# Third pair's scores one slot sooner, last results in separate tiles, the first pair's subtraction and sums inside ScalarE's exponential

## The chip, the core and the metric

The kernel runs on one core of a Trainium2 chip. The metric is device time in microseconds (us), of one launch. A core has engines that run side by side, each in the order of its own instruction list: TensorE (PE in the profile; its weight loads are PEld), VectorE (DVE), ScalarE (ACT), GpSimd (POOL, hardly used here), and SyncE (SP), which here only issues transfers. Matmuls write to PSUM; VectorE and ScalarE read it from there.

## What is computed

A chunked attention followed by a feed-forward layer with the Mish function, in float32:

```python
# attention: q, k, v are (8, 8, 576, 64); chunks of 64 positions
scores = scale * np.matmul(q_c, k_c.transpose(0, 1, 2, 4, 3))
scores = scores - np.max(scores, axis=-1, keepdims=True)
attn = np.exp(scores)
attn = attn / (np.sum(attn, axis=-1, keepdims=True) + 1e-09)
x = np.matmul(attn, v_c)           # then laid out as (4608, 512)
# feed-forward: w_in (512, 2048), w_out (2048, 512)
h = x @ w_in
g = h * np.tanh(softplus(h))       # Mish
out = g @ w_out                    # (4608, 512)
```

## The kernel before

**Tiles.** The 4608 tokens are worked in nine blocks of 512 (`NB`), the 2048 inner columns in sixteen slices of 128 (`NF`), so there are 144 steps `i` = block * 16 + slice. A block needs the attention of two *pairs* `j` (256 tokens each, eight heads); pairs 0 and 1 feed block 0, pairs 2 and 3 block 1, and so on. In the text the third pair is `j` = 2 and the fourth is `j` = 3.

**Feed-forward.** `up(i)` (L288) makes `h` in PSUM with twelve matmuls: x and the weights are split into a high part and a small rest (`xh`, `xl`, `wi_h`, `wi_l`), and three of the four products are added up. `mish(i)` (L300, ScalarE) makes `z`; `g_hi` (L306 on ScalarE for even steps of block 0, else L308 on VectorE) and `g_lo` (L313, VectorE) split it into `gh` and `gl`. `down(i)` (L326) adds twelve matmuls into four accumulators `acc[t]` of 128 tokens, three for each. Per token group it takes `gl`, then `wo_l`, then `wo_h`. After the sixteenth slice `store` copies them out (L344, L346) and issues the transfers (L351).

**Weights.** They come as 64-bit numbers and are converted once, slice by slice, in the first 115 us: `w_load` (SyncE), `w_scale` (ScalarE, L89 and L93), `w_bits` (VectorE, two instructions, L99), `w_hi` (ScalarE, L114), `w_lo` (VectorE, L117). `order` lists the slices: index 2s + 3 is the output slice `o` of step s, index 2s + 4 the input slice `i` of step s + 3. `w_scale(0)` means the first of that list.

**Attention of a pair.** `a_scores` (TensorE, L162), `a_max` (VectorE, L189), `a_sub` (VectorE, L201, writes `p`), `a_exp` (ScalarE, L210, in place), `a_inverse` (VectorE: the sum L215, then + 1e-9 and the reciprocal, L216, L217), `a_norm` (VectorE, L222), `a_transpose` (TensorE, L231, into `pt`), `a_copy` (ScalarE, L241), `a_values` (TensorE, `av`), `a_hi` (ScalarE, L262, writes `xh`) and `a_lo` (VectorE, L265, writes `xl`). Exponential and Mish need different tables, so ScalarE loads a table (ACT_TABLE_LOAD) ahead of a change from one to the other.

**Order.** It is written out by hand. `prologue()` does pairs 0 and 1, each in two halves (FIRST, SECOND) so that one half can follow the other through the engines; `keep_busy(n)` puts in matmuls on the identity whose result nobody reads (L361). Then come slots `s` = 0 to 142. A slot issues on TensorE `up(s + 1)`, transposes, values and scores of whichever pair is due, then `down(s - 1)`; on VectorE and ScalarE the split of `z`, two weight slices (list indices 2s + 3 to 2s + 6 in various steps) and the attention steps that are due. In the slot's first half stand `a_max`, `a_norm`, `a_copy`, `a_exp`; in its second half, after `mish(s + 1)`, stand `a_sub`, `a_inverse`, `a_lo`. `plan` says in which slot a step of a pair is due: pair j has a base slot k0 (1 for pair 2, 8 for pair 3), and scores are due at k0, maximum and subtraction at k0 + 1, exponential and sum at k0 + 2, normalisation at k0 + 3, transposes and copy at k0 + 4, values at k0 + 5, `xh` and `xl` at k0 + 6. VectorE and ScalarE take what is listed strictly in order, so a step that waits holds all that is listed behind it.

**PSUM.** Scores, transposes and values of the pairs share one place (`HOME`, tag `a`); `ps_h` holds two tiles `h`; `ps_o` holds two tiles `o0` and `o2`, each with two accumulators. The prologue uses `o0` and `o2` as further places. In the last block `down` of the last two steps is interleaved by token group, with `store` behind each group:

```python
for i, t in ((2, 0), (2, 1), (1, 0), (2, 2), (1, 1), (2, 3), (1, 2), (1, 3)):
    down(N - i, (t,))
    if i == 1:
        store(NB - 1, (t,), end=True)
```

Of the kernel before, what the change touches and what calls it, by code (L numbers as in the profile page):

```python
# [9 lines left out]
F32 = mybir.dt.float32  # L10
# [7 lines left out]
P = 128  # L18
# [5 lines left out]
def kernel(  # L24
# [183 lines left out]
    def a_exp(j, t=BOTH):  # L208
        p = st[j]["p"][:, t]
        nc.scalar.activation(out=p, in_=p, func=AF.Exp, scale=SCALE)  # L210

    def a_inverse(j, t=BOTH):
        p = st[j]["p"][:, t].rearrange("p t g c k -> p (t g) c k")
        r = small(j, "r", t)
        nc.vector.tensor_reduce(out=r.rearrange("p c n -> p n c"), in_=p, op=ALU.add, axis=AX.X)  # L215
        nc.vector.tensor_scalar(out=r, in0=r, scalar1=1e-9, scalar2=None, op0=ALU.add)  # L216
        nc.vector.reciprocal(out=r, in_=r)  # L217

# [98 lines left out]
    def down(i, ts=range(TOK // P)):  # L317
        b, f = divmod(i, NF)
        d = it[i]
        for t in ts:  # L320
            if f == 0 and t % 2 == 0:
                o = ps_o.tile([P, 2, DM], F32, name=f"o_{b}_{t}", tag=f"o{t}")
                acc[t], acc[t + 1] = o[:, 0], o[:, 1]
            sl = slice(t * P, (t + 1) * P)
            for n, (g, w_) in enumerate(((d["gl"], wo_h), (d["gh"], wo_l), (d["gh"], wo_h))):
                nc.tensor.matmul(  # L326
                    acc[t],
                    lhsT=g[:, sl],
                    rhs=w_[:, f],
                    start=(f == 0 and n == 0),  # L330
                    stop=(f == NF - 1 and n == 2),
                )

    def store(b, ts=range(TOK // P), end=False):

        for t in ts:
            o = wst.tile([P, DM, 2], U32, name=f"ob_{b}_{t}", tag="st", bufs=4)
            o = o.rearrange("p n t -> p (n t)")[:, :DM].bitcast(F32)
            if end and t == TOK // P - 1:
                half = DM // 2  # L340
                nc.vector.tensor_copy(out=o[:, :half], in_=acc[t][:, :half])
                nc.scalar.copy(out=o[:, half:], in_=acc[t][:, half:])
            elif t % 2:
                nc.vector.tensor_copy(out=o, in_=acc[t])  # L344
            else:
                nc.scalar.copy(out=o, in_=acc[t])  # L346
            pair, c = divmod(t, 2)
            for i in range(2):
                r = (b * 2 * PAIRS + pair * 2 + i) * P + c * CHUNK
                queue = nc.scalar if end and i else nc.sync  # L350
                queue.dma_start(out=out[r : r + CHUNK, :], in_=o[i * CHUNK : (i + 1) * CHUNK])  # L351
# [13 lines left out]
    def prologue():  # L365
# [13 lines left out]
        for t, place in (FIRST, HOME), (SECOND, O0):  # L379
            keep_busy(7 if t == FIRST else 3)  # L380
            a_scores(0, t, place)
            a_max(0, t)
            a_sub(0, t)
            a_exp(0, t)
        w("scale", 0)
        for t, place in (FIRST, O2), (SECOND, HOME):
            a_inverse(0, t)
            a_norm(0, t)
            keep_busy(9 if t == FIRST else 3)
            a_transpose(0, t, place)  # L390
            a_copy(0, t)
        w("bits", 0)
        w("hi", 0)
        w("lo", 0)
        for t, place in (FIRST, O0), (SECOND, O2):
            a_values(0, t, place)
        for t in FIRST, SECOND:
            a_hi(0, t)
            a_lo(0, t)
        w("scale", 1)  # L400
        for t, place in (FIRST, HOME), (SECOND, O0):
            a_scores(1, t, place)
# [2 lines left out]
            a_exp(1, t)  # L405
        w("scale", 2)
        w("load", 4)
        up(0, A)
        for t, place in (FIRST, O2), (SECOND, HOME):
            a_inverse(1, t)  # L410
            a_norm(1, t)
            keep_busy(8 if t == FIRST else 4)
            a_transpose(1, t, place)
            a_copy(1, t)
        w("bits", 1)
        w("hi", 1)
# [16 lines left out]
        load_qk(2)  # L433
        w("load", 6)

    plan = {}
    for j in range(PAIRS, NPAIR):
        b, i = divmod(j, PAIRS)
        k0 = (b - 1) * NF + 1 + 7 * i
        for n in range(-2, 7):  # L440
            plan.setdefault(k0 + n, {})[n] = j

    def slot(s):
        a = plan.get(s, {})
# [1 line left out]

        if 1 <= s and s + 1 < N:
            up(s + 1, last="w")
        if 4 in a:
            a_transpose(a[4])  # L450
        if 5 in a:
            a_values(a[5])
        if 0 in a:
            a_scores(a[0])
        if 1 <= s <= N:
            down(s - 1)

# [5 lines left out]
        w("scale", n + 2)  # L463
        w("bits", n + 1)
        w("lo", n)
        if 1 in a:
            a_max(a[1])
        if 3 in a:
            a_norm(a[3])
        if 4 in a:  # L470
            a_copy(a[4])
        if 2 in a:
            a_exp(a[2])

        w("load", n + 5)
        if 6 in a:
            a_hi(a[6])
        if s + 1 < N:
            mish(s + 1)
        w("hi", n + 1)  # L480
        w("scale", n + 3)
        w("bits", n + 2)
        w("lo", n + 1)
        if 1 in a:
            a_sub(a[1])
        if 2 in a:
            a_inverse(a[2])
        if 6 in a:
            a_lo(a[6])
        if -2 in a and a[-2] > 2:  # L490
            load_qk(a[-2])
        if 1 in a:
            load_v(a[1])
        if s >= 1 and s % NF == 0:
            store(s // NF - 1)

# [49 lines left out]
```

## Time and profile before

| | us |
|---|---|
| three runs | 876.34, 876.52, 877.51 |
| median | 876.52 |
| the profiled execution | 877.21 |
| its span, first to last instruction | 875.4 |
| TensorE busy | 861.2 (98% of the span) |
| VectorE busy | 342.6 (39%) |
| ScalarE busy | 253.9 (29%) |

The profile is of one execution. Busy shares are means over the whole span; stage by stage they differ, and VectorE and ScalarE are far busier in the first 115 us, while the weights are converted, than after. In a row of the timeline the first number is the start in us from the beginning of the span, the second how long it lasted, then come engine, line of the kernel, operation, what it writes and reads, shapes, a count where rows are merged, and in brackets how long the engine stood idle before it and what released it.

### The profile page before, as it was taken

Reading aid. Unit: us, or ns where it says so; the run is one execution under the profiler, and the core shown is the slowest. Engines: PE = TensorE matmul, PEld = TensorE weight load, DVE = VectorE, ACT = ScalarE, POOL = GpSimd, SP = SyncE. Lnnn points to the kernel's source line nnn. Section 1 sums busy time; section 2 is a strip of 40 time slices with the busy share of each in tenths; the row PEclk is TensorE's granted clock in tenths of the full one; section 3 lists DMA queues with packets and bytes.
Section 4 is the critical chain, followed back from the end, with each engine's and each line's share of the span. In section 5 each row is a group of like instructions: output and inputs, shape, how many; then the busy total and the mean of one; then the engine's idle time right before and its main releaser. Section 6 shows DMA issues by size and latency. Waiting matters only on the chain.

```text
span 875.4 us, 13641 instructions
## 1 busy us (share of the span) xinstructions
PE 861.2 (98%) x5984; PEld 709.0 (81%) x5984; DVE 342.6 (39%) x534; ACT 253.9 (29%) x361; POOL 0.7 (0%) x6
## 2 busy tenths in 40 slices
PE   7989999999999999999999999999999999999997
PEld 7778888888888888888888888888888888888885
DVE  6898854242334233323424242423242242422221
ACT  4887832121312112221213131212222131311111
POOL 0000000000000000000000000000000000000000
PEclk9999999999999999999999999999999999999999
DMA  7656512101210120112120121012111202002001
GB/s 265 218 191 225 186 42 56 49 25 49 73 49 25 49 73 25 49 27 55 40 68 9 47 73 49 25 50 73 28 46 49 56 19 72 1 1 49 1 0 49
DMA packets 25179, 55.40 MB, mean 63 GB/s; under 512 B 2592, under 2 KB 2592, under 8 KB 25120
## 3 DMA queue, kind: packets, MB, share of 16 engines
q1 hardware_dynamic: 24512, 53.49, 20.8%
q8 instruction: 47, 0.77, 0.4%
q10 hardware_dynamic: 608, 1.05, 0.3%
q14 instruction: 12, 0.10, 0.0%
HBM read 45.09 MB, written 9.44 MB: 62 GB/s over the span
## 4 chain that ended last, share of the span: by engine, by line
PE 91%; DVE 5%; ACT 3%; issue 1%; ACTq 0%; POOLq 0%; POOL 0%; DVEq 0%
PE o L326 43%; PE h L288 41%; PE s L162 2%; PE av L162 2%; PE pt L231 2%; DVE wic L99 1%; DVE woc L99 1%; DVE p L222 1%; DVE m L189 0%; DVE wo_l L117 0%; PE spare L361 0%; ACT L300 0%; DVE r L215 0%; DVE wi_l L117 0%; ACT L210 0%
## 5 line engine op out<-in xcount | busy, mean ns | idle before, releaser
L308 DVE CAST gh<-z 128x512 fp32r<-128x512 f32 x136 | 57.9, 426 | 470.0 <-PE o L326 470.0
L326 PE MATMUL o<-wo_h,gl 128*128 128x512 f32 x576 | 229.9, 399 | 0.7 <-ACT ob L346 0.7
L326 PE MATMUL o<-wo_l,gh 128*128 128x512 f32 x576 | 225.1, 391 | 0.1
L326 PE MATMUL o<-wo_h,gh 128*128 128x512 f32 x576 | 224.9, 391 | 0.0
L300 ACT ACTIVATE z<-h 128x512 f32<-128x512 f32 x144 | 86.0, 597 | 454.3 <-PE h L288 348.5
L288 PE MATMUL h<-xh,wi_l 128*128 128x512 f32 (+1 forms) x580 | 154.4, 388 | 0.9 <-ACT xh L262 0.9
L288 PE MATMUL h<-xl,wi_h 128*128 128x512 f32 (+1 forms) x580 | 154.1, 388 | 0.3 <-ACT z L300 0.3
L288 PE MATMUL h<-xh,wi_h 128*128 128x512 f32 (+1 forms) x580 | 154.2, 388 | 0.0
L326 PEld LDWEIGHTS o<-wo_h,gl 128*128 128x128 f32 x576 | 108.5, 188 | 25.1 <-ACT ob L346 1.5
L288 PEld LDWEIGHTS h<-xh,wi_l 128*128 128x128 f32 x580 | 108.4, 188 | 23.4 <-ACT xh L262 1.0
L326 PEld LDWEIGHTS o<-wo_h,gh 128*128 128x128 f32 x576 | 108.4, 188 | 22.9
L288 PEld LDWEIGHTS h<-xl,wi_h 128*128 128x128 f32 x580 | 108.2, 188 | 22.9 <-ACT z L300 0.7
L288 PEld LDWEIGHTS h<-xh,wi_h 128*128 128x128 f32 x580 | 108.5, 188 | 22.3
L326 PEld LDWEIGHTS o<-wo_l,gh 128*128 128x128 f32 x576 | 108.5, 188 | 21.5 <-DVE wo_l L117 0.5
L313 DVE TENSOR_TENSOR gl<-z,gh 128x512 fp32r<-128x512 f32 x144 | 99.7, 692 | 9.5 <-ACT gh L306 4.8
L241 ACT COPY ps<-pt 128x1024 f32<-128x1024 f32 (+1 forms) x20 | 18.6, 928 | 83.4 <-PE pt L231 83.4
L300 ACT ACT_TABLE_LOAD x17 | 21.8, 1283 | 34.5 <-PE h L288 34.5
L344 DVE COPY ob<-o 128x512 f32<-128x512 f32 x17 | 11.8, 692 | 35.5 <-ACT ob L346 32.8
L231 PE MATMUL pt<-ident,p 128*128 128x128 f32 x144 | 19.6, 278 | 5.6 <-DVE p L222 3.4
L189 DVE TENSOR_REDUCE m<-s 128x16 f32<-128x1024 f32 (+1 forms) x20 | 22.2, 1112 | 5.4 <-PE s L162 5.4
L231 PEld LDWEIGHTS pt<-ident,p 128*128 128x128 f32 x144 | 16.8, 142 | 8.9 <-issue 3.5
L201 DVE TENSOR_TENSOR p<-s,m 128x1024 f32<-128x1024 f32 (+1 forms) x20 | 22.3, 1117 | 0.6
(40 smaller groups left out, 380.0 us busy)
## 6 DMA issues: line engine op xcount, KB each, us to landing
out<-ob SPq DMA_DIRECT2D x68, 128.0 KB, 2.4
wis<-in_w_in SPq DMA_DIRECT2D x16, 512.0 KB, 4.2
wos<-in_w_out SPq DMA_DIRECT2D x16, 512.0 KB, 4.6
q<-in_q SPq DMA_DIRECT2D x16, 512.0 KB, 3.7
k<-in_k SPq DMA_DIRECT2D x16, 512.0 KB, 3.7
v<-in_v SPq DMA_DIRECT2D x16, 512.0 KB, 4.3
room_v<-in_v SPq DMA_DIRECT2D x2, 512.0 KB, 7.2
q<-in_q SPq DMA_DIRECT2D x2, 256.0 KB, 3.9
```

Of the source, the lines that this page charges most:

```text
L99: nc.vector.scalar_tensor_tensor(out=c, in0=x, scalar=mask, in1=d["a"][:, :, 0] if op == ALU.logical_shift_left else c, op0=op, op1=ALU.bi ...
L162: nc.tensor.matmul(o[h * CHUNK : (h + 1) * CHUNK, c, t - ts.start, g], lhsT=l[rows, t, 2 * g + h], rhs=r[rows, t, 2 * g + h], start=True, ...
L189: nc.vector.tensor_reduce(out=small(j, "m", t), in_=st[j]["s", t.start].rearrange("p c t g k -> p c (t g) k"), op=ALU.max, axis=AX.X,)
L201: nc.vector.tensor_tensor(out=d["p"][:, t].rearrange("p t g c k -> p c (t g) k"), in0=d["s", t.start].rearrange("p c t g k -> p c (t g) k" ...
L231: nc.tensor.transpose(out=d["pt", ts.start][:, t - ts.start, g], in_=d["p"][:, t, g].rearrange("p c k -> p (c k)"), identity=ident,)
L241: nc.scalar.copy(out=d["ps"][:, t].rearrange("p t h k -> p (t h k)"), in_=d["pt", t.start][:, : t.stop - t.start].rearrange("p t g n -> p ...
L288: nc.tensor.matmul(h[:, cols], lhsT=w_[:, f, kt], rhs=x[:, kt, cols], start=(n == 0), stop=(n == 3 * NK - 1),)
L300: nc.scalar.activation(out=d["z"], in_=d["h"], func=AF.Mish)
L308: nc.vector.tensor_copy(out=d["gh"], in_=d["z"])
L313: nc.vector.tensor_tensor(out=d["gl"], in0=d["z"], in1=d["gh"].bitcast(F32), op=ALU.subtract)
L326: nc.tensor.matmul(acc[t], lhsT=g[:, sl], rhs=w_[:, f], start=(f == 0 and n == 0), stop=(f == NF - 1 and n == 2),)
L344: nc.vector.tensor_copy(out=o, in_=acc[t])
```

## The change

Four things change. In the first pair the maximum `m` is multiplied by -SCALE, and ScalarE computes the exponential of each 64-wide group straight from the scores, with that as the bias and with the group's sum as a second output; subtraction and sum on VectorE are dropped there. Around it, `w_scale(0)` goes behind the first half's copy, and `w_hi(0)`, `w_lo(0)` behind `xh` and `xl`; `up(0, A)` takes its products in the opposite order, and the second pair has fewer `keep_busy`. For the other pairs `a_inverse` is only cut in two. In `plan`, the third pair's scores, maximum, subtraction, exponential, sum and normalisation, and the load of its `v`, come one slot earlier; its transposes, values and the rest stay where they were, and its `q` and `k` are still loaded at the prologue's end. A block's accumulator tiles are all taken at its first `down`; in the last block there are three, `o0`, `o2` and `HOME`, with groups 0 and 3 in `o0`. The last group is copied by ScalarE in one piece.

```diff
+    def a_exp_sum(j, t):
+        d = st[j]
+        m, r = d["m", t.start], small(j, "r", t)
+        if t.start == 0:
+            d["p"] = at.tile([P, 2, NG, 2, CHUNK], F32, name=f"p_{j}", tag="A")
+        nc.vector.tensor_scalar(out=m, in0=m, scalar1=-SCALE, scalar2=None, op0=ALU.mult)
+        for g in range(NG):
+            for c in range(2):
+                nc.scalar.activation(
+                    out=d["p"][:, t.start, g, c],
+                    in_=d["s", t.start][:, c, 0, g],
+                    func=AF.Exp,
+                    scale=SCALE,
+                    bias=m[:, c, g : g + 1],
+                    accum_out=r[:, c, g : g + 1],
+                )
+
+    def a_sum(j, t=BOTH):
+        p = st[j]["p"][:, t].rearrange("p t g c k -> p (t g) c k")
+        r = small(j, "r", t).rearrange("p c n -> p n c")
+        nc.vector.tensor_reduce(out=r, in_=p, op=ALU.add, axis=AX.X)
+
     def a_inverse(j, t=BOTH):
-        p = st[j]["p"][:, t].rearrange("p t g c k -> p (t g) c k")
-        r = small(j, "r", t)
-        nc.vector.tensor_reduce(out=r.rearrange("p c n -> p n c"), in_=p, op=ALU.add, axis=AX.X)
+        r = st[j]["r", t.start]
         nc.vector.tensor_scalar(out=r, in0=r, scalar1=1e-9, scalar2=None, op0=ALU.add)
         nc.vector.reciprocal(out=r, in_=r)
...
-            if f == 0 and t % 2 == 0:
-                o = ps_o.tile([P, 2, DM], F32, name=f"o_{b}_{t}", tag=f"o{t}")
-                acc[t], acc[t + 1] = o[:, 0], o[:, 1]
+            if f == 0 and t == 0:
+                places = [(ps_o, "o0"), (ps_o, "o2")] + ([HOME] if b == NB - 1 else [])
+                o = [p.tile([P, 2, DM], F32, name=f"o_{b}_{tag}", tag=tag) for p, tag in places]
+                n = len(o)
+                acc.update({u: o[u % n][:, u // n] for u in range(4)} if n == 3 else
+                           {u: o[u // 2][:, u % 2] for u in range(4)})
...
-            if end and t == TOK // P - 1:
-                half = DM // 2
-                nc.vector.tensor_copy(out=o[:, :half], in_=acc[t][:, :half])
-                nc.scalar.copy(out=o[:, half:], in_=acc[t][:, half:])
-            elif t % 2:
+            if t % 2 and not (end and t == TOK // P - 1):
                 nc.vector.tensor_copy(out=o, in_=acc[t])
             else:
                 nc.scalar.copy(out=o, in_=acc[t])
...
             a_scores(0, t, place)
             a_max(0, t)
-            a_sub(0, t)
-            a_exp(0, t)
-        w("scale", 0)
+            a_exp_sum(0, t)
         for t, place in (FIRST, O2), (SECOND, HOME):
             a_inverse(0, t)
             a_norm(0, t)
             keep_busy(9 if t == FIRST else 3)
             a_transpose(0, t, place)
             a_copy(0, t)
+            if t == FIRST:
+                w("scale", 0)
         w("bits", 0)
-        w("hi", 0)
-        w("lo", 0)
...
             a_hi(0, t)
             a_lo(0, t)
+        w("hi", 0)
+        w("lo", 0)
...
-        up(0, A)
-        for t, place in (FIRST, O2), (SECOND, HOME):
+        up(0, A, last="w")
+        for t in FIRST, SECOND:
+            a_sum(1, t)
             a_inverse(1, t)
             a_norm(1, t)
-            keep_busy(8 if t == FIRST else 4)
-            a_transpose(1, t, place)
+            keep_busy(6 if t == FIRST else 3)
+            a_transpose(1, t, O2 if t == FIRST else HOME)
             a_copy(1, t)
...
+    NAMES = ("load", "s", "max", "exp", "norm", "t", "v", "x")
     plan = {}
     for j in range(PAIRS, NPAIR):
         b, i = divmod(j, PAIRS)
         k0 = (b - 1) * NF + 1 + 7 * i
-        for n in range(-2, 7):
-            plan.setdefault(k0 + n, {})[n] = j
+        at_ = (-2, 0, 1, 2, 3, 4, 5, 6) if j > PAIRS else (-3, -1, 0, 1, 2, 4, 5, 6)
+        for name, n in zip(NAMES, at_):
+            plan.setdefault(k0 + n, {})[name] = j
```

In `slot` the numbers of the steps become these names, and `a_sum` stands ahead of `a_inverse`.

## Rows read from the trace of the kernel before

**Rows 1.** List of waits, TensorE: us in total, times, longest us

```profile
PE pt L231 <- DVE p L222: 3.4, 4, 2.5
PE o L326 <- ACT ob L346: 0.7, 1, 0.7
```

**Rows 2.** Table by stage: busy us of PE, PEld, DVE, ACT, POOL; PEclk; DMA

```profile
10.00:20.00 10.00, 7.81 (x170) 6.98 (x170) 9.01 (x18) 6.26 (x12) 0.00 (x0) 1.00 0.72 278
60.00:70.00 10.00, 10.00 (x99) 8.05 (x99) 9.22 (x16) 9.48 (x17) 0.00 (x0) 0.88 0.58 188
```

**Rows 3.** Timeline of TensorE, slots 4 and 5; last, `down(4)` from the chain

```profile
50.60 0.19 PEld L326 LDWEIGHTS o<-wo_l,gh 128*128 128x128 f32 x1 [0.50 <-DVE wo_l L117]
...
58.58 1.59 PE L231 MATMUL pt<-ident,p 128*128 128x128 f32 x8 [2.46 <-DVE p L222]
...
60.17 3.82 PE o L326 x12
```

**Rows 4.** Timeline of VectorE, slots 1 to 13

```profile
35.12 0.42 DVE L308 CAST gh<-z 128x512 fp32r<-128x512 f32 x1
...
60.28 0.42 DVE L308 CAST gh<-z 128x512 fp32r<-128x512 f32 x1
...
70.79 0.43 DVE L308 CAST gh<-z 128x512 fp32r<-128x512 f32 x1 [0.33 <-PE o L326]
...
82.99 0.43 DVE L308 CAST gh<-z 128x512 fp32r<-128x512 f32 x1 [1.49 <-PE o L326]
...
98.31 0.69 DVE L313 TENSOR_TENSOR gl<-z,gh 128x512 fp32r<-128x512 f32 x1
...
100.25 0.68 DVE L117 TENSOR_TENSOR wo_l<-woc,wo_h 128x512 fp32r<-128x512 f32 x1
...
109.08 0.42 DVE L308 CAST gh<-z 128x512 fp32r<-128x512 f32 x1
```

**Rows 5.** Timeline of TensorE, the fourth pair's transposes

```profile
102.21 1.06 PE L231 MATMUL pt<-ident,p 128*128 128x128 f32 x8 [0.22 <-DVE p L222]
```

**Rows 6.** Timeline of VectorE and, at 12.62, of ScalarE in the prologue

```profile
5.36 0.69 DVE L189 TENSOR_REDUCE m<-s 128x8 f32<-128x512 f32 x1 [5.36 <-PE s L162]
...
10.67 0.17 DVE L216 TENSOR_SCALAR r<-r 128x8 f32<-128x8 f32 x1
...
11.12 0.69 DVE L222 TENSOR_TENSOR p<-p,r 128x512 f32<-128x512 f32 x1
...
12.62 0.59 ACT L241 COPY ps<-pt 128x512 f32<-128x512 f32 x1 [1.18 <-PE pt L231]
...
14.43 1.28 DVE L265 TENSOR_TENSOR xl<-av,xh 128x512 fp32r<-128x512 f32 x2
...
15.63 0.68 DVE L189 TENSOR_REDUCE m<-s 128x8 f32<-128x512 f32 x1
```

**Rows 7.** Groups by line and form, ScalarE: count | busy us, mean ns | idle before

```profile
L210 ACT ACTIVATE p<-p 128x512 f32<-128x512 f32 x4 | 2.5, 630 | 6.4 <-DVE p L201 6.4
L342 ACT COPY ob<-o 128x256 f32<-128x256 f32 x1 | 0.4, 373 | 1.6 <-DVE ob L341 1.6
```

**Rows 8.** DMA issues, 20 to 36 us (last: us to landing); timeline of TensorE

```profile
q<-in_q SPq DMA_DIRECT2D x1, 512.0 KB, 5.7
...
29.63 0.73 PE L288 MATMUL h<-xl,wi_h 128*128 128x512 f32 x2 [0.29 <-ACT z L300]
```

**Rows 9.** Timeline of the last block's end, TensorE and ScalarE

```profile
866.97 0.19 PEld L326 LDWEIGHTS o<-wo_h,gl 128*128 128x128 f32 x1 [0.41 <-ACT ob L346]
...
869.37 0.59 ACT L346 COPY ob<-o 128x512 f32<-128x512 f32 x1 [2.45 <-PE o L326]
...
869.98 0.50 ACTq L351 DMA_DIRECT2D out<-ob  x1
...
870.00 0.50 PE L326 MATMUL o<-wo_h,gl 128*128 128x512 f32 x1 [0.70 <-ACT ob L346]
...
871.52 0.37 ACT L342 COPY ob<-o 128x256 f32<-128x256 f32 x1 [1.57 <-DVE ob L341]
```

More of the change, by code (lines that the diff above doesn't have):

```diff
@@ L448, in slot @@
             up(s + 1, last="w")
[L449 to L454, printed above, removed]
+        if "t" in a:
+            a_transpose(a["t"])
+        if "v" in a:
+            a_values(a["v"])
+        if "s" in a:
+            a_scores(a["s"])
         if 1 <= s <= N:
@@ L465, in slot @@
         w("lo", n)
[L466 to L473, printed above, removed]
+        if "max" in a:
+            a_max(a["max"])
+        if "norm" in a:
+            a_norm(a["norm"])
+        if "t" in a:
+            a_copy(a["t"])
+        if "exp" in a:
+            a_exp(a["exp"])
         w("load", n + 5)
-        if 6 in a:
-            a_hi(a[6])
+        if "x" in a:
+            a_hi(a["x"])
         if s + 1 < N:
@@ L483, in slot @@
         w("lo", n + 1)
[L484 to L493, printed above, removed]
+        if "max" in a:
+            a_sub(a["max"])
+        if "exp" in a:
+            a_sum(a["exp"])
+            a_inverse(a["exp"])
+        if "x" in a:
+            a_lo(a["x"])
+        if a.get("load", 0) > PAIRS:
+            load_qk(a["load"])
+        if "max" in a:
+            load_v(a["max"])
         if s >= 1 and s % NF == 0:
```

## Prediction, made before the change had run

> **What bounds the kernel now.** I read the page first, then the list of waits, then the table by stage, and only then the timeline of the stretches that these point to. TensorE is the bound of the whole, so a microsecond is won only where it stands idle or runs slowly. The list of waits gives its largest wait as the transposes' wait for VectorE's normalised `p`, 3.4 us in four times, 2.5 of them in one; the output copies hold it once in the whole span [rows 1]. The table by stage shows the stretch that follows that one wait with a granted clock of 0.88, a mixture of 2.4 and 1.2 GHz [rows 2]. The timeline shows three small places: the prologue, a chain that alternates between VectorE, ScalarE and TensorE [rows 6]; slots 4 and 5, where `down(3)` waits 0.50 us for `wo_l` and the third pair's transposes wait 2.46 us [rows 3]; and the end, where `down` waits for copies out of the same tile [rows 9]. All else is back-to-back matmul. The change touches just these three.
>
> **The prologue.** For each half of the first pair VectorE loses a subtraction and a sum, some 0.7 us each (maximum and normalisation of that size take 0.69), and gains a scaling of `m` of 128x8, 0.17 us long [rows 6]. ScalarE loses one exponential of 128x512, 0.63 us, and gains eight of 128x64, each with a pointer for the bias and a sum read out [rows 7]. The trace has no such instruction; call its spacing e. A copy of 256 columns takes 0.37 and an exponential of 512 takes 0.63 [rows 7], so about 1.0 ns a column and 0.12 us fixed; 64 columns make 0.18. From below: e = 0.12, if neighbours overlap and pointer and sum are free. From above: 0.18, the fixed part once more for the pointer, and a second instruction for the sum at the 0.24 between starts of VectorE's smallest steps (10.67 to 11.12 holds two [rows 6]), together 0.54. I take 0.30, a little under the middle, because small steps of one engine follow each other more closely than they last.
>
> The first maximum ends at 6.05 [rows 6] and the scaled `m` is there at about 6.25; sixteen exponentials then end at E = 6.4 + 16e. The second half's `+1e-9` and reciprocal take 0.45, as between 10.67 and 11.12 [rows 6], so its normalisation starts at E + 0.5 = 6.9 + 16e against 11.12: a shift of 16e - 4.2. From there the chain is the old one (transposes, copy at 12.62, values, `xh`, `xl`, next pair's maximum at 15.63 [rows 6]) with one edit: `w_hi(0)` and `w_lo(0)` go behind `xh` and `xl`. The second `xl` comes about 0.4 sooner after the copy, as ScalarE has no cast ahead of `xh`, and VectorE then spends 0.6 on `w_lo(0)` before the maximum: 0.2 later on balance. So the second pair, and all that VectorE does after it, moves by d = 16e - 4.0: it breaks even at e = 0.25, gives +0.8 us at 0.30, +3.2 at 0.45, and no better than about -0.9 for cheap ones, since then the first copy, the two passes of `w_scale(0)` and the second copy queue on ScalarE. `w_scale(0)` behind the first copy otherwise costs nothing: ScalarE would wait for the second transposes there. Nothing downstream absorbs d, because VectorE and ScalarE hand work to each other without a gap until `gl(0)`. Fewer `keep_busy` matmuls and `up(0)` begun with `xl` cost nothing: TensorE waits for VectorE behind them anyway.
>
> On the price of e a page speaks against this edit: in the Trainium skill, "ScalarE: Activation LUTs", section "What ACT_TABLE_LOAD costs", an ACTIVATE with a pointer bias is put at 280 ns + 0.833 ns a column with 93 ns of overlap, an estimate of 0.24 us for 64 columns, and its section "Rules for kernel authors" sends multiply and add to VectorE. By that figure d would be -0.2; what the read-out of the sum adds no run here shows.
>
> **The third pair.** Scores move from slot 1 to slot 0, maximum and subtraction from 2 to 1, the exponential and sums from 3 to 2, the normalisation from 4 to 3; the transposes stay in slot 5. The 2.46 us wait goes, as `p` is ready a slot earlier. What is late next? VectorE works through one in-order list, and the list of slots 1 to 5 is then, instruction for instruction, that of slots 9 to 13 in the trace of before, where the fourth pair has the same places (maximum in an odd slot, exponential in an even one). So I lay that stretch on this one. `gh(9)` starts at 82.99 and `gh(1)` at 35.12 [rows 4]; subtract 47.87. `gl(11)` at 98.31 to 99.0 becomes `gl(3)` until 51.13; `wo_l` at 100.25 to 100.93 becomes `wo_l(3)` until 53.06; the normalisation, which ended just ahead of the transposes at 102.21 [rows 5], ends at 54.2; `gh(13)` at 109.08 becomes `gh(5)` at 61.21, against 60.28 before [rows 4].
>
> TensorE reaches `down(3)` at about 50.1 as before (it began its second matmul at 50.60 after 0.50 of waiting [rows 3]). Now it waits for `gl(3)` until 51.2, does one matmul, and waits for `wo_l(3)` until 53.1: `down(3)` ends 2.5 us later than before, and the one wait has become two shorter ones. The transposes follow at about 58.4 against 58.58 [rows 3]: of the 2.46 us only 0.2 are left. What can remain is the clock: if the split waits don't lower it, the transposes take 1.06 [rows 5] in place of 1.59 [rows 3] and `down(4)` its usual 2.7 in place of 3.8 [rows 3], together 1.6, so TensorE enters slot 6 about 1.8 earlier. VectorE, however, is 0.93 later at `gh(5)`. It has idle time of 0.33 and 1.49 us ahead of `gh(7)` and `gh(9)` [rows 4] in which it waited for TensorE; used up, that makes it 0.89 earlier, and the fourth pair's transposes, which already waited 0.22 for it [rows 5], can't start earlier than that. Gain: 0.9 without a clock dip, 0.1 with one. I take 0.9: the waits are 1.0 and 1.6 long, and the prologue, where TensorE idles 2.2 us in 10 in shorter pieces, kept its full 2.4 GHz [rows 2].
>
> The scores in slot 0 need `k`, which is issued just behind `q`; `q` took 5.7 us to land [rows 8], so `k` lands near 30 and not at 29.35, when TensorE is free. They fill the 0.29 us wait ahead of `up(2)` [rows 8] and may add 0.5 of their own; the wait at `down(3)` swallows both. `load_v(2)` goes a slot ahead on SyncE's queue, behind `w_load(10)` and ahead of `w_load(11)`; 512 KB more there delay a weight that ScalarE wants a slot later: nothing.
>
> **The last block.** `acc` 0 to 3 get three tiles, so `down` of tile 1 no longer waits for the copy of tile 0 (0.41 between weight loads [rows 9], about 0.2 more than usual), nor that of tile 3 for the copy of tile 2 (start 870.00, where nine matmuls at 0.23 from 866.97 would give 869.15 [rows 9]): TensorE ends about 1.0 sooner. The last copy is one of 0.59 on ScalarE in place of two halves one after the other, but it stands behind the copy of tile 2 and that copy's 0.50 issue [rows 9]: 869.2 + 0.6 + 0.5 + 0.6 = 870.9 against 871.89, where the second half ended [rows 9]. Gain 1.0 (0.7 if the closer transfers land more slowly, 1.3 if issuing doesn't hold the engine). Taking both tiles of a block at its first matmul costs nothing at the earlier borders, where the copies were never waited for [rows 1].
>
> **The sum.** Prologue +0.8, third pair -0.9, end -1.0: -1.1 us. The profiled execution took 877.21 us, 1.81 of it around a span of 875.4; so 874.3 + 1.8 = 876.1 for its like. It stands 0.69 above the median, 876.52; from that, 875.4. A measurement can tell about 0.2% from no change, 1.75 us here, so this is "no change", on its better side.
>
> **The rivals.** (1) Cheap exponentials: with e between 0.12 and 0.25 d lies between -0.9 and 0 and the time between 873.7 and 874.6. For it speaks the small slope and fixed part of [rows 7], against it that pointer and sum have to cost something. (2) Dear exponentials, slower: it is the read-out of the sum as a second instruction that doesn't overlap. At 0.48 the sum passes +1.8, and it is slower by over 0.2% from there on (from 0.43 with the clock dip of rival 4). At 0.50 d is 4.0 and the time 878.6 to 879.4. (3) The wait really goes: VectorE keeps up, `down(3)` doesn't wait, and the 2.46 us with the 1.6 of slow clock come in full: 876.5 + 0.8 - 4.0 - 1.0 = 872.3. Against it speaks [rows 4], where the same instruction list took 19.1 us. (4) The split waits lower the clock as the single one did: 876.2, the forecast's neighbour; in that case the change only moves its wait.
>
> **How the numbers follow.** Forecast with e from 0.25 to 0.40, without the dip 0.28 (875.4) and with it, rival 4, 0.20; together from 874.6 to 877.8. Rival 1: 0.20. Rival 2, e above 0.40: 0.21. Rival 3: 0.10. Remainder 0.01. Faster by over 0.2%, below 874.8: rivals 1 and 3 and a little of the forecast, 0.34. Slower, above 878.3: rival 2 without its lower end, 0.18. The same: 0.48. The range that leaves out 2 in 10 goes from 872.9 to 878.8.
>
> **What would show it.** On ScalarE the sixteen exponentials, start to start; VectorE's maximum of the second pair at 15.63 + d; waits of TensorE in slot 4 (`gl`, then `wo_l`) and none at the third pair's transposes; a wait of about 1.1 us at the fourth pair's; granted clock of the stretch from 50 to 62; at the end no wait for `ob`, and the last copy at about 870 less the earlier shift. If the third pair's wait vanishes and no wait appears in slot 4, the laying of one stretch on another is wrong; if the maximum comes at 14 or at 19, only e is.

## The result and the profile after

The changed kernel took 878.64 us (median of 21 runs, 877.55 to 880.18) against 876.89 for the kernel before in runs beside it (21 runs, 876.34 to 878.93): a ratio of 1.0017, 95% interval 1.0011 to 1.0023. By that ratio it is about 1.5 us slower, where 1.1 faster was forecast. The time lies just below the upper end of the range, 878.8, but not for the reason that set that end. The profiled execution of the changed kernel took 879.15 with a span of 877.4.

The timeline of ScalarE at the start, first in the changed kernel (columns as in the rows above; L221 is the exponential with bias and sum, L262 and L283 the copies of `pt` and `xh`):

```profile
6.82 1.28 ACT L221 ACT_TABLE_LOAD   x1 [6.82 <-DVE m L218]
8.11 0.32 ACT L221 ACTIVATE p<-s,m 128x64 f32<-128x64 f32 x1
8.32 0.19 ACT L221 ACTIVATION_READ_ACCUMULATOR p<-s,m 128x1 f32 x1
8.42 0.31 ACT L221 ACTIVATE p<-s,m 128x64 f32<-128x64 f32 x1
...
12.67 0.29 ACT L221 ACTIVATION_READ_ACCUMULATOR p<-s,m 128x1 f32 x1
```

and in the kernel before:

```profile
1.66 1.28 ACT L210 ACT_TABLE_LOAD   x1 [1.66 <-PEq L536]
6.81 0.63 ACT L210 ACTIVATE p<-p 128x512 f32<-128x512 f32 x1 [3.86 <-DVE p L201]
```

Two things are to be seen. One exponential with its read-out follows the other every 0.29 to 0.31 us. And the table load, which stood at 1.66 while ScalarE had nothing to do, now waits for VectorE's scaled `m` and lies on the path: `m` releases it at 6.82, and the first exponential starts at 8.11. In the kernel before the exponential itself starts at 6.81, its table loaded long before.

VectorE in the changed kernel: the first maximum, the second half's normalisation, the second pair's maximum, `gh(1)`, the weight slice ahead of which it idles, `gh(5)` and `gh(9)`. They answer to [rows 4] and [rows 6]:

```profile
5.84 0.69 DVE L189 TENSOR_REDUCE m<-s 128x8 f32<-128x512 f32 x1 [5.84 <-PE s L162]
...
13.43 0.69 DVE L243 TENSOR_TENSOR p<-p,r 128x512 f32<-128x512 f32 x1
...
19.17 0.68 DVE L189 TENSOR_REDUCE m<-s 128x8 f32<-128x512 f32 x1
...
39.17 0.42 DVE L329 CAST gh<-z 128x512 fp32r<-128x512 f32 x1
...
51.85 0.69 DVE L117 TENSOR_TENSOR wi_l<-wic,wi_h 128x512 fp32r<-128x512 f32 x1 [1.55 <-ACT wi_h L114]
...
65.24 0.42 DVE L329 CAST gh<-z 128x512 fp32r<-128x512 f32 x1
...
85.84 0.42 DVE L329 CAST gh<-z 128x512 fp32r<-128x512 f32 x1
```

The second pair's maximum is at 19.17 in place of 15.63, and `gh(1)` 4.05 us later than before. From there on the lateness shrinks again. Of the 4.05 us 0.48 stand at the first maximum already (5.84 against 5.36 [rows 6]), which waits for TensorE: the 32 matmuls of the first scores took 1.13 us from 4.64 on, in the kernel before 0.69 from 4.60 on.

TensorE in the changed kernel, the waits of the prologue, of slots 0 to 5 and of the fourth pair:

```profile
11.90 0.63 PE L252 MATMUL pt<-ident,p 128*128 128x128 f32 x4 [1.73 <-ACT p L221]
...
14.27 1.09 PE L252 MATMUL pt<-ident,p 128*128 128x128 f32 x4 [1.07 <-DVE p L243]
...
23.80 0.63 PE L252 MATMUL pt<-ident,p 128*128 128x128 f32 x4 [2.00 <-ACT wis L93]
...
34.66 1.16 PE L162 MATMUL s<-k,q 64*64 64x64 f32 x64 [1.23 <-DMA k<-in_k]
...
55.32 0.47 PE L351 MATMUL o_o<-wo_h,gl 128*128 128x512 f32 x1 [0.21 <-DVE gl L334]
...
57.16 0.50 PE L351 MATMUL o_o<-wo_l,gh 128*128 128x512 f32 x1 [1.37 <-DVE wo_l L117]
...
62.53 1.03 PE L252 MATMUL pt<-ident,p 128*128 128x128 f32 x8
...
105.05 1.06 PE L252 MATMUL pt<-ident,p 128*128 128x128 f32 x8 [0.33 <-DVE p L243]
```

The third pair's wait of 2.46 us is gone, and `down(3)` waits for `gl` and then `wo_l` in its place. In the prologue the same four transposes take 0.63 us once and 1.09 another time. The table by stage says why (columns as in [rows 2]; the number ahead of the DMA share is the granted clock):

```profile
12.50:15.00 2.50, 1.43 (x11) 1.22 (x9) 1.48 (x4) 2.06 (x7) 0.00 (x0) 0.83 1.06 416
15.00:17.50 2.50, 2.50 (x86) 2.21 (x87) 1.37 (x3) 1.33 (x3) 0.00 (x0) 0.50 0.22 84
...
22.50:25.00 2.50, 1.20 (x8) 1.23 (x9) 2.30 (x7) 1.64 (x4) 0.00 (x0) 0.87 0.00 0
25.00:27.50 2.50, 2.50 (x41) 1.99 (x42) 2.43 (x5) 0.91 (x3) 0.00 (x0) 0.50 0.00 0
```

After the waits of 1.73 and 1.07 us, and again after the one of 2.00, TensorE ran at 1.2 in place of 2.4 GHz; the kernel before has 1.00 in all of its prologue ([rows 2] shows 10 to 20).

At the end the last copy, by ScalarE in one piece, ends at 873.79, where the kernel before ended at 871.89 [rows 9]:

```profile
873.20 0.59 ACT L367 COPY ob<-o_o 128x512 f32<-128x512 f32 x1 [0.70 <-PE o_o L351]
```

So the lateness in this execution is 4.05 behind the prologue, 2.84 at the fourth pair's transposes (105.05 against 102.21 [rows 5]) and 1.90 at the last copy: the third pair gave 1.2 and the end 0.94.

### The profile page after: what moved, and what is told of

It is laid out like the page before. It is cut to its first block, busy times and chain, and to the rows that moved or that the text cites. A ratio compares the mean times of both kernels' runs of the same rounds, so it can differ in the third digit from the quotient of the medians.

```text
span 877.4 us, 13655 instructions
## 1 busy us (share of the span) xinstructions
PE 861.9 (98%) x5978; PEld 710.9 (81%) x5978; DVE 339.8 (39%) x531; ACT 258.2 (29%) x391; POOL 0.7 (0%) x6
## 3 DMA queue, kind: packets, MB, share of 16 engines
q10 hardware_dynamic: 608, 1.05, 0.3%
## 4 chain that ended last, share of the span: by engine, by line
PE 90%; DVE 4%; ACT 4%; issue 1%; ACTq 0%; POOLq 0%; POOL 0%
PE o_o L351 41%; PE h L309 41%; PE av L162 2%; PE pt L252 2%; PE s L162 2%; PE o_a L351 1%; DVE woc L99 1%; DVE wic L99 1%; DVE wo_l L117 1%; ACT p L221 1%; PE spare L382 1%; DVE m L189 0%; ACT L321 0%; DVE wi_l L117 0%; ACT woc L89 0%
## 5 line engine op out<-in xcount | busy, mean ns | idle before, releaser
L351 PE MATMUL o_o<-wo_h,gl 128*128 128x512 f32 x560 | 223.0, 398 | 0.2 <-DVE gl L334 0.2
L351 PE MATMUL o_o<-wo_l,gh 128*128 128x512 f32 x560 | 218.4, 390 | 1.4 <-DVE wo_l L117 1.4
L351 PE MATMUL o_o<-wo_h,gh 128*128 128x512 f32 x560 | 218.3, 390 | 0.0
L351 PEld LDWEIGHTS o_o<-wo_h,gl 128*128 128x128 f32 x560 | 105.1, 188 | 23.4 <-ACT z L321 0.6
L351 PEld LDWEIGHTS o_o<-wo_l,gh 128*128 128x128 f32 x560 | 105.2, 188 | 22.1 <-DVE wo_l L117 1.7
L351 PEld LDWEIGHTS o_o<-wo_h,gh 128*128 128x128 f32 x560 | 105.1, 188 | 22.1
L262 ACT COPY ps<-pt 128x1024 f32<-128x1024 f32 (+1 forms) x20 | 18.7, 935 | 82.4 <-PE pt L252 82.4
L321 ACT ACT_TABLE_LOAD x17 | 21.8, 1283 | 34.5 <-PE h L309 34.5
L365 DVE COPY ob<-o_o 128x512 f32<-128x512 f32 x17 | 11.8, 691 | 35.6 <-ACT ob L367 33.2
L162 PEld LDWEIGHTS s<-k,q 64*64 64x64 f32 x1088 | 17.9, 137 | 7.7 <-issue 7.0
```

The source lines that it names most:

```text
L162: nc.tensor.matmul(o[h * CHUNK : (h + 1) * CHUNK, c, t - ts.start, g], lhsT=l[rows, t, 2 * g + h], rhs=r[rows, t, 2 * g + h], start=True, ...
L262: nc.scalar.copy(out=d["ps"][:, t].rearrange("p t h k -> p (t h k)"), in_=d["pt", t.start][:, : t.stop - t.start].rearrange("p t g n -> p ...
L321: nc.scalar.activation(out=d["z"], in_=d["h"], func=AF.Mish)
L351: nc.tensor.matmul(acc[t], lhsT=g[:, sl], rhs=w_[:, f], start=(f == 0 and n == 0), stop=(f == NF - 1 and n == 2),)
```

## The experiments

Theory A, from the traces: the exponentials cost what was forecast; the prologue lost 1.3 us to the table load and over a microsecond to the lowered clock; third pair and end gave what was forecast. Rival theory B: the exponential part costs by something else (its instructions, the new place of weight steps). Rival C: the third pair or the end gave less than forecast.

**The three parts alone.** The kernel before with one part each: in `plan` the third pair's six steps from scores to normalisation a slot sooner; the separate tiles with the whole last copy; the first pair's exponential with the reordering around it.

```diff
-            plan.setdefault(k0 + n, {})[n] = j
+            early = 1 if j == PAIRS and n <= 3 else 0
+            plan.setdefault(k0 + n - early, {})[n] = j
```

> The kernel before with nothing but the third pair's scores to normalisation one slot sooner. Theory A (the move pays little, because VectorE's list then holds TensorE in slot 4): 0.9 us faster than before, 1.2 at most (ratio 0.9986 to 0.9990); gh(9) starts without the 1.49 us of idle time; TensorE waits about 2.5 us at down(3) and about 1 us at the fourth pair's transposes. Theory B (the loss of the whole change lies in this move): slower than before by 1 us or more. Theory C (the 2.46 us wait and the slow clock behind it come back in full): 4 us faster (ratio 0.9955).

> The kernel before with nothing but the separate accumulator tiles and the last copy in one piece. Theory A: 0.9 to 1.0 us faster (ratio 0.9989), no wait of TensorE for the output copies, last copy ending 0.9 to 1.0 us sooner in the span. Rival: the closer transfers at the end land more slowly and take it back, no difference.

> The kernel before with nothing but the first pair's change (exponentials with bias and sum, and the moves around them). Theory A (all of the loss lies here): 3.5 to 4.1 us slower (ratio 1.0040 to 1.0047), the second pair's first maximum at 19 instead of 15.6, clock below 1 between 12 and 18 and between 24 and 28 us. Theory B (the loss lies in the third pair's move): within 1 us of the kernel before.

Measured: third pair alone 0.9993 (0.9984 to 1.0002), end alone 0.9991 (0.9982 to 1.0000), exponential alone 1.0017 (1.0008 to 1.0026). Third pair and end gave about 0.6 and 0.8 us. Both intervals, some 0.8 us to either side, hold what was forecast, and the first holds zero too, so these two runs alone don't refute C; the profiles speak against it. In the profile of the third pair alone `gl(0)` came 1.3 us later than before (the first maximum stood at 5.84, and the second pair's at 16.72), TensorE then waited 1.8 for `k`, and yet the fourth pair's transposes were only 0.13 late; in the profile of the end alone the last copy ended 0.82 sooner. The two rows, one of each kernel:

```profile
102.34 1.06 PE L231 MATMUL pt<-ident,p 128*128 128x128 f32 x8 [0.34 <-DVE p L222]
```

```profile
870.49 0.58 ACT L346 COPY ob<-o_o 128x512 f32<-128x512 f32 x1 [0.70 <-PE o_o L330]
```

The exponential alone cost 1.5 us, less than half of what I expected of it. Its prologue was late by 3.05 at `gl(0)`, as theory A has it, but by the fourth pair's transposes only 1.4 was left. Its table by stage and its third pair's transposes:

```profile
12.50:15.00 2.50, 2.33 (x11) 2.06 (x10) 1.41 (x4) 2.12 (x7) 0.00 (x0) 0.50 1.04 406
...
60.00:65.00 5.00, 3.38 (x19) 2.99 (x20) 4.93 (x8) 3.77 (x7) 0.00 (x0) 1.00 0.49 151
```

```profile
61.62 1.06 PE L252 MATMUL pt<-ident,p 128*128 128x128 f32 x8 [2.47 <-DVE p L243]
```

The wait of 2.47 us was there as before, but the clock was 1.00 behind it and the transposes took 1.06 in place of 1.59 [rows 3]. That gave 1.6 back. My expectation had priced the lowered clock behind that wait as certain; it isn't.

**The table loaded early.** The changed kernel with one exponential of one column ahead of the first maximum, so that the load has no wait in front of it:

```diff
         load_qk(0, None, (FIRST, SECOND), (nc.sync, nc.scalar))
+        warm = const.tile([P, 1], F32, name="warm")
+        nc.vector.memset(warm, 0.0)
+        nc.scalar.activation(out=warm, in_=warm, func=AF.Exp)
```

> The changed kernel with one exponential of a single zeroed column ahead of everything on ScalarE, so that its table is loaded in the first 3 us and not behind the wait of the first real exponential. Theory A (the load behind the wait lies on the path): 1.3 us faster than the changed kernel, so 877.3 or 0.4 us slower than before (ratio 1.0005); if the clock then stays at 2.4 GHz in the prologue, up to 2.5 us faster than the changed kernel (876.1, ratio 0.999). Rival (the load is hidden beside VectorE's and TensorE's work): no difference from the changed kernel, ratio 1.002.

Measured 1.0220 (1.0206 to 1.0234), 19 us slower than the kernel before, though the prologue did as expected: the load stood at 1.66, the first exponential at 6.90 and the second pair's maximum at 16.94. The groups by line and form show where the 19 us are, in every large matmul (count | busy us, mean ns | idle), first this kernel, then the changed one:

```profile
L309 PE MATMUL h<-xh,wi_l 128*128 128x512 f32 x572 | 156.7, 395 | 0.0
```

```profile
L309 PE MATMUL h<-xh,wi_l 128*128 128x512 f32 x572 | 152.9, 389 | 0.0
```

In the chain of waits twelve of `down`'s matmuls took 2.80 here and 2.72 there, so a matmul starts every 0.233 in place of 0.227 us; over some 3,400 of them that is about the loss. What was new besides the early load was a tile of four bytes a partition in the kernel's first pool, ahead of the tiles of all other pools. So the same was done again with that tile in a pool behind all others:

```diff
+    last = ctx.enter_context(tc.tile_pool(name="last", bufs=1))
...
-        warm = const.tile([P, 1], F32, name="warm")
+        warm = last.tile([P, 1], F32, name="warm")
```

> The changed kernel with the early table load again, the extra column now in a pool behind all others, so that no other tile changes its place in SBUF. Theory A: the matmuls start 0.227 us apart as before (12 in 2.72 us), the second pair's first maximum comes near 16.4 to 16.9 instead of 19.2, and the time is 2 to 3 us under the changed kernel's, 0.7 to 1.2 us under the kernel before (ratio 0.9986 to 0.9992). Rival: the early load or the extra exponential itself slows the matmuls as in the run before; then 897 again.

Measured 0.9998 (0.9989 to 1.0007), 1.7 us under the changed kernel's ratio; the twelve matmuls took 2.72 again. The early table thus takes back all that the change had lost. Not all of it is the load: TensorE's first two waits are 1.16 and 1.07 us in this profile, in place of 1.73 and 1.07, and the granted clock stays at 1.00 from 10 to 20 us. The early exponential and load cost nothing, ScalarE being idle. What is still missing to the forecast shows in its table by stage:

```profile
20.00:22.50 2.50, 1.56 (x9) 1.59 (x10) 2.36 (x7) 1.39 (x3) 0.00 (x0) 0.77 0.00 0
22.50:25.00 2.50, 2.50 (x63) 2.14 (x64) 2.43 (x5) 1.16 (x3) 0.00 (x0) 0.55 0.13 8
```

**The clock kept up.** The changed kernel with more matmuls on the identity in its waits:

```diff
-            keep_busy(9 if t == FIRST else 3)
+            keep_busy(16 if t == FIRST else 7)
...
-            keep_busy(6 if t == FIRST else 3)
+            keep_busy(12 if t == FIRST else 4)
```

> The changed kernel with more matmuls on the identity in the prologue's gaps (16 and 7 for 9 and 3, 12 and 4 for 6 and 3), nothing else; the table load stays late. Theory A (the lowered clock after the gaps has a part of its own): clock 1.00 from 10 to 30 us, the second pair's first maximum at 18.2 instead of 19.2, 1 to 1.5 us faster than the changed kernel (877.3, ratio 1.0003). Rival (the clock costs nothing because VectorE is the bound): same time as the changed kernel, ratio 1.002.

Measured 1.0003 (0.9994 to 1.0012), 1.2 us under the changed kernel's ratio. The granted clock was 1.00 in every stretch of the prologue, and `gl(0)` stood at 33.27 in place of 34.70, 1.43 sooner. The mean clock over the span, which is on record for each run, agrees. Of the changed kernel's 21 runs fifteen stand at 0.996 or less (thirteen at 0.996, with a median of 878.70 us) and six at 0.998 (877.55 to 877.90); here nine of eleven stand at 0.999 or 1.000. The mean doesn't tell where in the span the clock fell. The table by stage does:

```profile
12.50:15.00 2.50, 2.32 (x24) 1.99 (x26) 1.39 (x4) 2.15 (x7) 0.00 (x0) 1.00 1.05 410
...
25.00:27.50 2.50, 1.61 (x67) 1.17 (x65) 2.43 (x5) 2.17 (x5) 0.00 (x0) 1.00 0.25 49
```

**Both.** The early table and the busy TensorE together:

> The changed kernel with both undone that were left out of the sum: the one-column exponential early, in a tile behind all others (the table is loaded before the first maximum), and more matmuls on the identity in the waits of the prologue (the clock stays up). If these two are all that was missed, the second pair's maximum comes at d = 0.8 (16.4 after an ordinary start, 0.5 later after a slow one), gl(0) comes about 0.8 later than in the kernel before (31.4), the granted clock is 1.00 throughout the prologue, and the time is the forecast's: ratio 0.998 to 0.9995, at or a little under the run with the table alone (0.9998). If a third cause is at work in the prologue, gl(0) stays above 32 with a clock of 1.00 everywhere and the ratio above 1.000.

Measured 0.9988 (0.9979 to 0.9996). VectorE's maxima and the first `gl` of its profile (the line numbers of this kernel are one higher than those of the changed one):

```profile
5.53 0.69 DVE L190 TENSOR_REDUCE m<-s 128x8 f32<-128x512 f32 x1 [4.67 <-PE s L163]
...
16.59 0.68 DVE L190 TENSOR_REDUCE m<-s 128x8 f32<-128x512 f32 x1
...
31.61 0.69 DVE L335 TENSOR_TENSOR gl<-z,gh 128x512 fp32r<-128x512 f32 x1 [2.37 <-ACT gh L328]
```

It started 0.17 later than the kernel before (5.53 against 5.36 [rows 6]); less that, the second pair's maximum is 0.79 later than the 15.63 of before. The forecast's d was 0.8, and its ratio, 875.4 to 876.52, was 0.9987. So these two causes are all that the sum had left out, to within the interval of some 0.8 us, and B falls. C finds no support here either: with d at 0.8, third pair and end must have given some 1.9 for the whole to be 1.05 faster. The granted clock was 1.00 in every stretch up to 30 us. It was 0.73 from 30 to 35, behind a wait of 2.01 us for `k`, but TensorE then had no wait left at `down(3)`, so that this loss came out of time that the changed kernel spends waiting.

**Without the exponential part.** Third pair and end together; then the same with one more edit, which brings the second `w_hi` of a slot with an exponential in front of Mish and its table load:

```diff
-        if 2 in a:
+        exp_here = 2 in a
+        if exp_here:
             a_exp(a[2])
+            w("hi", n + 1)
...
-        w("hi", n + 1)
+        if not exp_here:
+            w("hi", n + 1)
```

> The changed kernel without the first pair's part: the kernel before with the third pair's move and the separate accumulator tiles. Theory A (the two parts add up): 1.7 to 2.1 us faster than before (ratio 0.9976 to 0.9981). If they do not add up, 1 us.

> As the run before it, and in the slots with an exponential the weight cast w_hi(n + 1) stands ahead of mish, between the two table loads, and not behind them. Theory A (in those slots VectorE idles 1.55 us because w_hi stands behind the second table load, and VectorE's list is what holds TensorE at down(3) and at the fourth pair's transposes): the 1.55 us idle times vanish, the wait at down(3) falls from 1.3 us to about 0, the fourth pair's wait as well; 1 to 2 us faster than the run before it (ratio 0.996 to 0.997). Rival (VectorE's idle time there costs nothing): same as the run before it.

Measured 0.9989 (0.9980 to 0.9998) and 0.9958 (0.9946 to 0.9970; median 873.25). The first is about half as good as expected, 1.0 us in place of 1.7 to 2.1, and its interval leaves out the 1.9 that were forecast for the two parts. Its profile tells why in part: `gl(0)` stood at 31.89, 1.25 late after a first maximum at 5.84, and the last copy ended at 871.04, 0.85 sooner than before, so third pair and end gave 2.1 behind a late prologue. How many of the executions begin late is not on record. The second is a little better than expected and faster than both kernels. What it removes is seen in the changed kernel's row at 51.85: VectorE idles 1.55 us for a `wi_h` that stands behind Mish and its table load on ScalarE. With the edit that idle time is gone in both slots, `down(3)` waits for nothing, and neither pair's transposes wait. Its TensorE:

```profile
31.50 1.29 PE L162 MATMUL s<-k,q 64*64 64x64 f32 x64 [1.94 <-DMA k<-in_k]
...
58.77 1.03 PE L231 MATMUL pt<-ident,p 128*128 128x128 f32 x8
...
100.40 1.03 PE L231 MATMUL pt<-ident,p 128*128 128x128 f32 x8
```

The edit alone, in the kernel before:

> The kernel before with one edit alone: in slots with an exponential, the second w_hi stands between exponential and Mish. VectorE's idle time ahead of w_lo in those slots (0.64 at 52.51, and the 1.49 at 82.99 that it leaves room for) should go, the third pair's transposes then wait 1.8 in place of 2.46, the fourth pair's 0.22 goes: ratio 0.9985 to 0.9995. If the edit is what made the combined version faster by itself, the ratio is 0.9975 or below; if it is worth nothing without the earlier slot, it is 1.0000.

Measured 0.9990 (0.9982 to 0.9999), as expected in size. But not by the way that I gave for the third pair: its transposes still waited 2.48, without a lowered clock behind (the first row), and the fourth pair's didn't wait (the second). Alone it gives 0.9 us; on top of the third pair's earlier slot and the separate tiles it gives 2.7 (0.9989 to 0.9958): there `down(3)` had waited 1.20 and the fourth pair's transposes 0.35, and with it neither waits. Where the other 1.1 come from the two profiles don't settle, since one begins a microsecond later than the other (`gl(0)` at 31.89 and 30.88). The profile of the edit alone shows one thing more: the old prologue, with all its matmuls on the identity, had a lowered clock too, 0.79 and 0.53 from 17.5 to 22.5 us, after TensorE had stood still for most of the 2.5 us before.

```profile
60.77 1.06 PE L231 MATMUL pt<-ident,p 128*128 128x128 f32 x8 [2.48 <-DVE p L222]
...
102.44 1.03 PE L231 MATMUL pt<-ident,p 128*128 128x128 f32 x8
```

**The scores left in slot 1.** The wait for `k` at 31.50 suggested to leave the scores behind `up(2)` and move only the five steps behind them:

```diff
-            early = 1 if j == PAIRS and n <= 3 else 0
+            early = 1 if j == PAIRS and 1 <= n <= 3 else 0
```

> The version with w_hi placed ahead of Mish (third pair a slot sooner, separate tiles, no change to the first pair), but with the third pair's scores left in slot 1 behind up(2); maximum, subtraction, exponential, sum and normalisation stay a slot sooner. There TensorE stood 1.94 us for k at the scores and went on at half rate; with up(2) ahead of the scores it does not stand, and is 3.3 us earlier at down(0) (33.7 in place of 37.0). VectorE's list is unchanged and its wo_l(3) and wo_l(4) were ready 1.9 us ahead of need, so 1.9 of the 3.3 are kept and 1.4 come back as a wait at down(3): ratio 0.9930 to 0.9945, against 0.9958 with the scores in slot 0. If the maximum now waits for scores, or if VectorE was the bound already, the ratio stays at 0.9955 or above.

Measured 0.9959 (0.9947 to 0.9972), the same as with the scores in slot 0; the expected further gain is not there. In the profile it is partly: no wait for `k`, a wait of 0.40 at `down(3)`, and the third pair's transposes at 57.08 in place of 58.77.

```profile
51.72 0.50 PE L330 MATMUL o_o<-wo_l,gh 128*128 128x512 f32 x1 [0.40 <-DVE wo_l L117]
...
57.08 1.03 PE L231 MATMUL pt<-ident,p 128*128 128x128 f32 x8
```

The profiled execution with the scores in slot 0 took 874.47, 1.2 us over the median of its kernel, and had a lowered clock behind the wait for `k` (0.74 from 30 to 35 us). I had taken that execution for the usual one. The mean clock of its five runs settles part of it: two of the other four stand at 1.000 (873.01 and 873.08 us) where the profiled one stands at 0.998, so in these the clock was higher. Whether the wait for `k` was shorter in them isn't settled: only one execution of each kernel was profiled.

## Why the prediction was wrong

**The price of the exponentials: right.** e was taken as 0.30 between 0.12 and 0.54; it is 0.29. Of this, 0.19 to 0.21 lie between an exponential and its read-out, 0.10 between the read-out and the next exponential. The rival "dear exponentials" ends at the measured time by accident: it wanted e at 0.48 or more. On the page that I cited (the Trainium skill, "ScalarE: Activation LUTs", "What ACT_TABLE_LOAD costs"): the estimate of 0.24 us from its figures was over the measured 0.20 for the exponential, and the read-out that it doesn't price took the difference back and 0.05 more. Its figure of 1283 ns for the load agrees with the row (1.28); the 1.38 us of draining that it adds does not show here: the load ends at 8.10 and the exponential starts at 8.11.

**The prologue's sum: wrong, by two terms that were not in it.** The failing step is "sixteen exponentials then end at E = 6.4 + 16e". It let them start when `m` was there, and it never asked where the table load in front of the first one would stand. The old exponential waited for VectorE alone and the load in front of it for nothing; the new one waits for VectorE and, reading the scores from PSUM, for TensorE too. The list of a line's instructions (durations in ns, then first and last start) shows where the wait for VectorE went, first in the changed kernel, then in the kernel before:

```profile
L221 ACTq EVENT_SEMAPHORE  x2: 17/17/17, 6.8 to 9.0; - x2
```

```profile
L210 ACTq EVENT_SEMAPHORE  x1: 38/38/38, 14.9 to 14.9; - x1
```

In the changed kernel a waiting instruction of its own, on VectorE's semaphore, stands at 6.8 straight ahead of the load, and the exponential at 8.11 carries TensorE's. In the kernel before nothing waits ahead of the load at 1.66, and the exponential at 6.81 carries VectorE's itself. So the load is held until `m` is there, and 1.3 us are lost (8.11 against 6.82). That it was the second wait that took the first out of the exponential and put it ahead of the load is argued from this; the runs show that the load comes early again, and that 1.7 us return, when another exponential stands ahead. The second missing term is the clock. "Fewer `keep_busy` matmuls ... cost nothing: TensorE waits for VectorE behind them anyway" priced these matmuls by the time that they take and not by what they hold up. The clock fell to 1.2 GHz twice, and 1.43 us went by `gl(0)`: first in the first pair, where nine and three stand as before but the waits had grown (1.73 and 1.07 us against 1.19 and 0.47), then in the second, where they were fewer (a wait of 2.00 against 1.00). The prediction never asked what clock the new prologue would have. That the old one kept 2.4 GHz [rows 2] it used only as a reason why the split waits of the third pair wouldn't lower it; for the prologue itself this would have held for the old gaps alone. The terms add up for the profiled execution: 0.8 as forecast (0.79 where both were undone), 1.3, 1.43, and 0.48 of a later start (first maximum at 5.84 against 5.36 [rows 6], which kernels with and without the change show by turns) make 4.01; measured at `gh(1)` 4.05.

**The third pair: right in its mechanism, 0.3 too small in the trace.** Laying slots 9 to 13 on slots 1 to 5 gave 26.09 us from `gh(1)` to `gh(5)`; it took 26.07. Both waits at `down(3)` were there, though shorter than forecast (0.21 and 1.37 for 1.0 and 1.6), the third pair's wait was gone and the clock between 50 and 62 stayed up (1.00 in the profile), as the forecast chose against rival 4. The scores waited 1.23 for `k`, and the stretch swallowed it. The fourth pair's transposes waited 0.33, not 1.1, and the stretch gave 1.2, not 0.9: VectorE used up 2.1 us of idle time between `gh(5)` and `gh(9)` where I counted 1.82. By all runs the part alone gave 0.6, with an interval that holds 0.9. Rival 3, the whole wait, did not come. The run with `w_hi` ahead of Mish came part of the way: 3.7 us under the kernel before (0.9958), where rival 3's 4.0 and the end's 1.0 make 5.0. What had stood against it was in the template, between `gh(9)` and `gh(13)`, in a row of the kernel before that [rows 4] leaves out:

```profile
95.67 0.69 DVE L117 TENSOR_TENSOR wi_l<-wic,wi_h 128x512 fp32r<-128x512 f32 x1 [1.54 <-ACT wi_h L114]
```

It is the same idle time as that at 51.85 in the changed kernel, 1.55. I laid it on slot 3 with the rest of the stretch and never asked what caused it. The 1.49 ahead of `gh(9)` that I counted as room is another one: there VectorE waits for TensorE.

**The end: right.** 1.0 forecast; 0.94 in the profile after, 0.82 in that of the part alone, 0.8 by all runs. No wait for a copy was left.

**The sum.** With the two missing terms the forecast would have been 875.4 + 1.3 + 1.4 = 878.1, and the measured ratio puts the time at 878.0 on the scale of the 876.52 it started from. It is closer than the parts allow: alone and by all runs the exponential part cost 1.5 and not 0.8 + 1.3 + 1.4 = 3.5, in part because the clock held behind the third pair's wait, as in its profile, and third pair and end together gave 1.0 and not 1.9. These two make 0.5, where the whole lost 1.5; intervals of 0.5 to 0.9 us on each can hide that difference. The range reached that far only because dear exponentials had been given 0.21; the mechanisms that came true had been given nothing.

## What to carry to other kernels

When an instruction on ScalarE changes its inputs, look at the table load ahead of it as at an instruction of its own: where it stands now, what it would wait for then, and whether a small activation earlier can draw it out of the path. A dummy matmul in a wait is priced by the clock of what follows, not by its own time; here nine and three of them sufficed before the waits grew, and no longer did after. And when one stretch of a trace serves as the template for another, ask of each idle time in it what causes it: the template carries its faults along, and removing one of them was worth more here than the whole change.

## What was not expected of the hardware

- A tile of four bytes a partition in the first pool, ahead of the tiles of all other pools, slowed every large matmul from 0.227 to 0.233 us (ratio 1.0220), and the same tile behind all others did not (0.9998). That the places of the operands in SBUF are the cause is argued from this pair of runs; which operand, and what about its place, stays open. The Trainium skill, "SBUF — State Buffer", "Specifications (TRN2)", says that an access pays for each crossing into a new line of 16 bytes. Where the tiles lay no run here shows.
- The same wait of 2.46 to 2.48 us ahead of the third pair's transposes was followed by a clock lowered to a mean of 0.88 over ten us in the kernel before [rows 2], and by 1.00 in two other kernels, the exponential alone and the moved `w_hi` alone, though waits of 1.07 to 2.00 us in the changed prologue were followed by 0.50. The executions of one kernel differ as well: of 27 of the kernel before, run beside the three parts, ten have a mean clock of 0.999 and took 876.29 to 877.19 us, the others 0.996 to 0.998 and 877.45 to 879.12; the profiled one, with the lowered clock, has 0.998. A wait's length alone doesn't tell what the clock will do.
